# Low rows of batch 0 as unfolded matmuls, and weights before x of batch 2, in an attention and Fourier-mixing kernel

## The chip, the cores and the metric

The kernel runs on one core of one Trainium2 chip. The metric is device time in microseconds (us) of one execution; lower is better. Before the change it took 301.66 us, the median of three runs (300.98, 301.66 and 306.95).

## The reference: what is computed

For each of 8 batches and 8 heads, with x of 512 rows by 64 and a state of 32 rows by 64, two attention reads are made without further projections, put below each other to 544 rows, and the heads side by side to 512 columns. Then comes a Fourier mixing layer with a residual, a normalization and a two-layer network:

```python
a     = softmax(x @ state.T / 8);  xread = a @ state      # 512 rows
a2    = softmax(state @ x.T / 8);  sread = a2 @ x         # 32 rows
X     = concat(xread, sread), heads side by side          # 8 x 544 x 512
u     = X + real(fft(fft(X, axis=1), axis=2))
un    = (u - mean(u)) / sqrt(var(u) + 1e-6)               # over the 512 columns
out   = u + relu(un @ w_ch1) @ w_ch2                      # 512 -> 2048 -> 512
```

## The kernel before, in words

**The transform.** The real part of the two Fourier transforms is made by matmuls with tables of cosines and sines. Symmetry is used twice: rows that mirror each other are added and subtracted ("folded") so that only about half of the row table is needed, and columns are folded again into four quarters (index j = 0 to 3; j = 0 and 1 go with cosines, TC, and j = 2 and 3 with sines, TS). Tiles XF and XR hold the forward and the reversed rows of the reads, in two groups k of 128 rows. The first 32 rows of XR[:, 0] are the "low rows": 32 rows that hold the low end of the sequence and later, written over them, the 32 rows of sread (state_rows). The low rows are folded by themselves: XT is a copy of them, XEl and XOl the sums and differences, XQl[:, j] the four quarters. The second row group of the tables, TC[:, 1] and TS[:, 1], belongs to them. sine_low (L258) writes cosines into rows 32 to 64 of TS[:, 1], which one extra row of XQl needs.

**The opening (batch 0).** open_batch and the batch-0 form of transform are written out by hand, in the order of the lines from L1003 on; each engine runs its instructions in that order. x of batch 0 is loaded and cast to bf16, turned by TensorE (turn_x0, the copies on ScalarE for blocks 0 and 1 and VectorE for 2 and 3), multiplied with the state (score), passed through exp on ScalarE, and read (read, sread). warm(n) issues n matmuls of 128 columns whose result nobody reads. The low rows of batch 0 are folded on GpSimd by low() (L655 to L662). even(k) and odd(k) fold the other rows on VectorE; NC and NS are the negated tables; terms_of(j, part) issues the matmuls of quarter j into the accumulators acc[j] ("gp"), terms_of(j, "low") those of the low rows (4 matmuls of 288 columns in all). out_of copies an accumulator to G; over_d multiplies G with the column table TEO ("yp", L669 and L670). TEO is made on ScalarE by second_sines and second_halves (L264, L268, L269). Then the sums with the reads, the centred rows ub, their turn into unT (turn_u), and layer 1 of batch 0 in 16 quarter steps L[0] to L[15] (L915).

**Batch 1 and the weave.** Between those quarter steps stand the steps of the attention of batch 1: s1 (scores) and r1 (reads), then its transform t1. r1 before the change is, by index: 0 read_low, 1 sread_heads, 2 fold_low (GpSimd), 3 read of rows 0, 4 an early VectorE add of row group 0 plus the GpSimd fold, 5 read of rows 128, 6 state_rows, 7 the last read and fold(). From L1151 on, weave() merges streams of steps by fractions: each stream is given a start and an end between 0 and 1, and its steps are spread evenly between them. M is layer 2 of batch 0 (L969), scores_next the scores of batch 2.

**Transfers.** Nearly all plain transfers are issued by SP's queue, in program order: x of batch b in seven pieces (L140), the states, DMA transposes of x and state for batches 2 and later (xT, sT; turned[b]), and the stores. The weights w1 and w2 are cast from f32 by transfers that GpSimd triggers, four each (L302, L310). A "gate" is a tiny GpSimd operation that reads a tile so that what follows it on GpSimd, or a load that reuses its buffer, comes no earlier. Before the change x of batch 2 is loaded as soon as w1 has landed (L1096), and w2 is triggered after x of batch 2 has landed (L308), in two pairs. States 3 to 7 are loaded into a part of gen2, a buffer that layer 1 of batch 1 takes over as hT.

The softmax here doesn't subtract the row's maximum and nothing guards it: scores larger than these inputs give would overflow.

## Time and profile before

| | |
|---|---|
| runs | 301.66 us (300.98 to 306.95) |
| the profiled execution | 306.59 us, its span 304.8 us |
| TensorE busy | 286.5 us (94%), 2312 matmuls |
| VectorE, ScalarE, GpSimd busy | 181.0, 135.6, 91.3 us |
| first matmul of layer 1, batch 0 | 23.59 us |
| TensorE's last terms matmul, opening | ends 19.97 us; first yp at 20.68 us |
| transfers of weights, trigger to landing | 6.0 to 18.2 us (median 13.2) |
| transposes of xT, batch 2 (four) | SP busy with them 37.06 to 52.6 us |

The profiled execution is one execution on the chip, and its clock times count from the start of its span. A group's line shows engine, line, operation, the tiles written and read, and the time of one. A wait is the idle time of an engine ahead of an instruction, with what ended it. PE is TensorE, DVE VectorE, ACT ScalarE, POOL GpSimd, SP SyncE, which issues transfers.

### The profile page before, as it was taken

The page shows a single profiled execution, that of the slowest core. Times are in us where ns is not written, and L with a number is a line of the kernel's source. Part 1 is how long each engine was busy: PE and PEld are TensorE (multiplying, and loading weights), DVE is VectorE, ACT ScalarE, POOL GpSimd, SP SyncE. Part 2 cuts the span into 40 slices and gives each one's busy share as a digit, 9 for nine tenths or more (in the row PEclk, how much of TensorE's full clock was granted, in tenths as well). Part 3 has the DMA queues.
Part 4 walks back from the last instruction along what each step waited for, and adds up shares of the span by engine and source line. Part 5 has one row for each costly group of instructions (what it writes and reads, how often), then busy time and mean ns, then how long its engine had stood idle before and what let it go on. Part 6 is the DMA issues. An engine that isn't in the chain of part 4 may idle for free.

```text
span 304.8 us, 6036 instructions
## 1 busy us (share of the span) xinstructions
PE 286.5 (94%) x2312; PEld 164.0 (54%) x2343; DVE 181.0 (59%) x443; ACT 135.6 (44%) x254; POOL 91.3 (30%) x217
## 2 busy tenths in 40 slices
PE   5989895799999999999999999999999999999996
PEld 4769792445544555456544555445444544555443
DVE  6876787658688395773827566684668484100012
ACT  5878561565543553345443445245523442333300
POOL 5982744391263033500406022701340031000000
PEclk9999999999999999999999999999999999999999
DMA  8998699974933975459252594363343023600355
GB/s 154 202 204 170 112 149 101 179 159 88 187 96 61 188 146 100 100 93 223 38 129 64 132 178 88 80 127 71 80 96 69 37 69 86 128 12 34 71 134 142
DMA packets 110794, 34.86 MB, mean 114 GB/s; under 512 B 101950, under 2 KB 106302, under 8 KB 110766
## 3 DMA queue, kind: packets, MB, share of 16 engines
q1 hardware_dynamic: 100046, 28.72, 49.0%
q0 software_dynamic: 4224, 4.19, 9.3%
q10 hardware_dynamic: 6496, 1.57, 2.5%
q8 instruction: 18, 0.29, 0.4%
q14 instruction: 10, 0.08, 0.1%
HBM read 22.41 MB, written 14.02 MB: 120 GB/s over the span
## 4 chain that ended last, share of the span: by engine, by line
PE 78%; DMA 11%; SPq 4%; POOL 3%; issue 1%; DVE 1%; ACT 1%; ACTq 0%; POOLq 0%; DVEq 0%
PE po L969 35%; PE ph L905 34%; DMA xT<-xin 5%; SPq L140 3%; DMA s_dram<-in_state_dram 3%; DMA xs<-in_x_dram 3%; PE gp L764 2%; PE po L961 1%; PE yp L669 1%; PE yp L670 1%; POOL w L310 1%; PE xfp L440 1%; PE xrp L440 1%; PE esp L415 1%; PE eTp L427 1%
## 5 line engine op out<-in xcount | busy, mean ns | idle before, releaser
L969 PE MATMUL po<-w,hT 128*128 128x512 bf16 x478 | 121.9, 379 | 5.0 <-DMA w<-in_moe_w_ch_dram 3.6
L907 ACT ACTIVATE hT<-ph 128x512 bf16<-128x512 f32 x112 | 66.8, 597 | 118.5 <-PE ph L905 116.4
L905 PE MATMUL ph<-unT,w 128*128 128x512 bf16 x435 | 112.7, 379 | 0.7
L905 PEld LDWEIGHTS <-w 128*128 128x128 bf16 x576 | 50.6, 98 | 47.4 <-issue 0.4
L969 PEld LDWEIGHTS <-hT 128*128 128x128 bf16 x496 | 46.9, 98 | 50.4 <-issue 4.0
L936 DVE SCALAR_TENSOR_TENSOR ot<-po,rstd,U 128x512 f32<-128x512 f32 (+2 forms) x33 | 24.2, 733 | 53.1 <-PE po L969 51.0
L768 POOL COPY GL<-G 128x128 bf16<-128x128 bf16 x7 | 2.0, 291 | 73.4 <-ACT G L765 73.4
L674 DVE TENSOR_TENSOR U<-yp,XR 128x512 f32<-128x512 f32 x14 | 9.6, 685 | 24.3 <-PE yp L670 24.3
L326 POOL TENSOR_TENSOR rstd<-mv,epst 128x1 f32<-128x1 f32 x34 | 6.7, 196 | 55.1 <-DVE mv L322 55.1
L320 DVE BATCH_NORM_STATS2 st<-U 128x6 f32<-128x512 f32 x32 | 21.7, 679 | 0.0
L327 POOL TENSOR_TENSOR rstd<-rstd,mhalf 128x1 f32<-128x1 f32 x34 | 20.1, 590 | 2.7
L915 PE MATMUL ph<-unT,w 128*128 128x128 bf16 x256 | 16.3, 219 | 0.3 <-ACT unT L835 0.3
L143 POOL CAST xin<-xs 128x512 bf16<-128x512 f32 (+1 forms) x12 | 15.1, 1280 | 2.5 <-DMA xs<-in_x_dram 2.4
L765 ACT CAST G<-gp 128x288 bf16<-128x288 f32 x28 | 13.2, 484 | 5.7 <-PE gp L764 5.7
L915 PEld LDWEIGHTS <-w 128*128 128x128 bf16 x256 | 14.8, 98 | 0.8 <-issue 0.6
L823 DVE TENSOR_SCALAR ub<-U,mv 128x512 bf16<-128x512 f32 x24 | 12.3, 514 | 0.9
L917 ACT ACTIVATE hT<-ph 128x512 bf16<-128x512 f32 x16 | 9.5, 596 | 6.4 <-PE ph L915 6.4
L1001 PE MATMUL warm<-ident 128*128 128x128 bf16 x70 | 7.4, 249 | 3.5 <-POOL xs L287 3.5
L497 POOL COPY XT<-XR 32x514 bf16<-32x514 bf16 x6 | 3.6, 603 | 21.7 <-DVE XR L449 21.7
L449 DVE TENSOR_TENSOR XR<-xrp,rs 128x512 bf16<-128x512 f32 x14 | 9.7, 694 | 0.5
L449 DVE TENSOR_TENSOR XF<-xfp,rs 128x512 bf16<-128x512 f32 x14 | 9.7, 691 | 0.5
L420 ACT ACTIVATE E<-esp 128x512 bf16<-128x512 f32 x14 | 8.4, 599 | 2.6 <-PE esp L415 2.6
(235 smaller groups left out, 371.6 us busy)
## 6 DMA issues: line engine op xcount, KB each, us to landing
xs<-in_x_dram SPq DMA_DIRECT2D x22, 256.0 KB, 3.9
w<-in_moe_w_ch_dram POOLq DMA_DIRECT2D x8, 512.0 KB, 13.2
out_dram<-ot SPq DMA_DIRECT2D x15, 256.0 KB, 3.4
r_dram<-ot SPq DMA_DIRECT2D x14, 256.0 KB, 2.3
out_dram<-r_dram SPq DMA_DIRECT2D x14, 256.0 KB, 3.5
xs<-in_x_dram SPq DMA_DIRECT2D x8, 192.0 KB, 4.8
xs<-in_x_dram ACTq DMA_DIRECT2D x2, 256.0 KB, 5.6
l_dram<-ot SPq DMA_DIRECT2D x2, 256.0 KB, 2.0
```

The source lines that it names most:

```text
L143: copy(xin_bufs[b % 2][:, lo:hi, 1:513], xs_of[b].rearrange("p (i c) -> p i c", i=4)[:, lo:hi])
L320: nc.vector.bn_stats(st6, u)
L327: nc.gpsimd.tensor_tensor(rstd, rstd, mhalf, op=ALU.pow)
L449: nc.vector.tensor_tensor(ov, in0=p[ps, :, 0:256].rearrange("p g (h d) -> p g h d", d=D), in1=rs[ps].unsqueeze(3).to_broadcast([n, 2, 4, D ...
L674: nc.vector.tensor_add(u.rearrange("p (k r) -> p k r", r=2), p.rearrange("p (r k) -> p k r", r=2)[:, 0:u.shape[1] // 2, :], x.rearrange("p ...
L765: nc.scalar.copy(G[:, j, :].rearrange("p (i q) -> p q i", q=2), p[:, 0:NM].rearrange("p (q i) -> p q i", q=2))
L823: nc.vector.tensor_scalar(t, in0=ud, scalar1=mv[:, 0:1], scalar2=None, op0=ALU.subtract)
L905: nc.tensor.matmul(ph[:, o:o + n], lhsT=w1[:, c, f * 128:(f + 1) * 128], rhs=un_of[key][:, c, :], start=(c == 0), stop=(c == DC - 1))
L907: nc.scalar.activation(hT[:, per * i:per * i + per, :].rearrange("p a b -> p (a b)"), ph, AF.Relu, scale=-1.0 / 512 if key == 0 else -1.0 ...
L915: nc.tensor.matmul(ph[:, o:o + 128], lhsT=w1[:, c, f * 128:(f + 1) * 128], rhs=un_of[key][:, c, 128 * r:128 * r + 128], start=(c == 0), st ...
L936: nc.vector.scalar_tensor_tensor(ot[:, cols], in0=po_of[i][:, 0:cols.stop - cols.start], scalar=rstd, in1=u[:, cols], op0=ALU.mult, op1=AL ...
L969: nc.tensor.matmul(po_of[i], lhsT=h_of[key][:, f, i * 128:(i + 1) * 128], rhs=w2[:, f, :], start=(f == 0), stop=(f == FC - 1))
```

## The change

The low rows of batch 0 are no longer folded. A copy XB holds them in order (XB[:, 0], by VectorE) and reversed (XB[:, 1], by GpSimd), with rows 32 to 64 zero, and low_of(j, sign) adds them to the accumulators by matmuls of shifted pieces with the plain or the negated table: 7 for j = 0 and 1 with the plain one, 6 for j = 2 and 3 (two of them of one column), and 8 with the negated. NC and NS now cover both row groups and lie in a work buffer. In the opening, fewer warms are issued, block 1 of x is copied by VectorE, score(1) gets a buffer of tag "t", second_table moves up and sine_low moves behind second_halves. w2 is triggered right behind w1. x of batch 1 is cast after odd(0). For batch 1 the early VectorE add is gone (fold adds both row groups) and the reads stand at other places among the quarter steps. x of batch 2 is loaded behind a gate on the third quarter of w2, and cast behind a gate on the last quarter of the folded rows. The other gates and moves are in the diff. States 3 to 7 get a buffer of their own tag (hTL), and their blocks are made in the weave of batch 1.

```diff
+    stl = wk.tile([128, 1024], F32, name="gen3", tag="hTL", bufs=1)[:, 0:640].rearrange("p (b g d) -> p b g d", b=5, g=2)
+    def states(lo, hi):
+        return stf[:, lo:hi] if lo < 3 else stl[:, lo - 3:hi - 3]
...
+    XB = wk.tile([128, 2, 514], F32, name="XB", tag="U", bufs=5)[0:64].rearrange("p a c -> p (a c)")[:, 0:514].bitcast(BF16).rearrange("p (a c) -> p a c", a=2)
-    NC, NS = [singles.tile([128, NM], BF16, name=n) for n in ("NC", "NS")]
+    NN = wk.tile([128, 2, 514], F32, name="NN", tag="U", bufs=5).rearrange("p a c -> p (a c)")[:, 0:2 * NM].bitcast(BF16)
+    NC, NS = [NN[:, 2 * NM * i:2 * NM * i + 2 * NM].rearrange("p (k c) -> p k c", k=2) for i in range(2)]
+    def minus(o, i):
+        nc.vector.tensor_scalar(o, in0=i, scalar1=-1.0, scalar2=None, op0=ALU.mult)
...
     def clears(i):
         if i == 0:
+            nc.gpsimd.memset(XB[32:64].rearrange("p a c -> p (a c)").bitcast(F32), 0.0)
...
+    def second_weights():
+        for q in range(4):
+            nc.gpsimd.dma_start(out=w2[:, q * 4:(q + 1) * 4, :], in_=w2v[:, q * 4:(q + 1) * 4, :])
-    def load_w2(lo, hi):
-        if lo == 0:
-            nc.gpsimd.tensor_copy(gate, xs_of[2][:, 0:2048:512])
-        for q in range(lo, hi):
-            nc.gpsimd.dma_start(out=w2[:, q * 4:(q + 1) * 4, :], in_=w2v[:, q * 4:(q + 1) * 4, :])
...
         def fold():
-            fold_rows(slice(1, 2) if b < 2 else slice(0, 2))
+            fold_rows(slice(0, 2))
...
         if b < 2:
-            second = [read_low, sread_heads, fold_low, read(0, False, XF[:, 0, 0:512]),
-                      lambda: (fold_rows(slice(0, 1)), fold_low_again()),
-                      read(128, False, XF[:, 1, 0:512]), state_rows,
+            second = [read_low, fold_low, fold_low_again, read(0, False, XF[:, 0, 0:512]), sread_heads,
+                      read(128, False, XF[:, 1, 0:512]), state_rows,
                       lambda: (read(256, True, XR[:, 1, 1:513])(), fold())]
...
-            return lambda: (nc.vector.tensor_copy if si > 1 else nc.scalar.copy)(
+            return lambda: (nc.vector.tensor_copy if si else nc.scalar.copy)(
...
-            p = es[si] = ps0.tile([128, 512], F32, name="esp", tag="e", bufs=2)
+            p = es[si] = ps0.tile([128, 512], F32, name="esp", tag="t" if si == 1 else "e", bufs=2)
...
+        def low_of(j, sign):
+            t, m = XB[:, 0], XB[:, 1]
+            table = ((TC, TS) if sign > 0 else (NC, NS))[j // 2][0:64, 1, :]
+            ws = ({1: [t[:, 0:128], m[:, 1:129], m[:, 257:385], t[:, 256:384]], -1: [t[:, 256:257]]},
+                  {1: [t[:, 0:128], m[:, 1:129], t[:, 256:257]], -1: [m[:, 257:385], t[:, 256:384]]},
+                  {1: [m[:, 1:129], m[:, 257:385]], -1: [t[:, 0:128], t[:, 256:384], t[:, 512:513]]},
+                  {1: [t[:, 384:512], m[:, 129:257]], -1: [m[:, 385:513], t[:, 128:256]]})[j][sign]
+            for w in ws:
+                nc.tensor.matmul(acc[j][0:w.shape[1], 0:NM], lhsT=w, rhs=table, start=False, stop=False)
+            if j == 2 and sign > 0:
+                for c in (128, 384):
+                    nc.tensor.matmul(acc[j][0:1, 0:NM], lhsT=t[:, c:c + 1], rhs=TC[0:64, 1, :], start=False, stop=False)
...
     turn_state()
-    warm(8)
+    second_table()
+    warm(5)
...
     exp2()
-    warm(4)
     copy = turn_x0(0)
...
     read(3)
-    nc.vector.tensor_copy(XTs[0], XRs[0][0:32, 0, :])
-    low()
-    state_blocks(1, 2, nc.gpsimd.tensor_copy)
-    for i in range(4):
-        cast_x(1, lo=i, hi=i + 1)
-    clears(1)
-    warm(6)
+    nc.vector.tensor_copy(XB[0:32, 0], XRs[0][0:32, 0, :])
+    nc.gpsimd.tensor_copy(XB[0:32, 1], XRs[0][0:32, 0, ::-1])
+    second_weights()
+    warm(4)
     read(1)
...
     begin()
-    warm(10)
+    warm(4)
+    low_of(0, 1), low_of(1, 1)
     state_rows()
-    sine_low()
     second_sines()
     second_halves()
-    warm(6)
+    sine_low()
+    low_of(2, 1), low_of(3, 1)
     even(1)
-    nc.vector.tensor_scalar(NC, in0=TC[:, 0, :], scalar1=-1.0, scalar2=None, op0=ALU.mult)
+    minus(NC, TC)
     terms_of(0, 1), terms_of(1, 1)
     odd(1)
-    nc.vector.tensor_scalar(NS, in0=TS[:, 0, :], scalar1=-1.0, scalar2=None, op0=ALU.mult)
-    terms_of(0, "low"), terms_of(1, "low")
+    minus(NS, TS)
+    low_of(0, -1), low_of(1, -1)
     terms_of(2, 1), terms_of(3, 1)
     even(0)
+    low_of(2, -1), low_of(3, -1)
     terms_of(0, 0)
     out_of(0)
     terms_of(1, 0)
     odd(0)
-    terms_of(2, "low"), terms_of(3, "low")
+    nc.gpsimd.tensor_copy(gate, XO0s[:, 0, 0:4])
+    for i in range(4):
+        cast_x(1, lo=i, hi=i + 1)
+    state_blocks(1, 2, nc.gpsimd.tensor_copy)
     terms_of(2, 0)
...
     keep_low()
+    clears(1)
     clear_state(2, 3)
     state_blocks(2, 3, nc.gpsimd.tensor_copy)
     make_mirror()
-    nc.gpsimd.tensor_tensor(gate, xs_of[0][:, 0:4], w1[:, :, 3 * 512], op=ALU.add)
-    load_x(2)
+    clear_state(3, B)
     turned[2, 0]()
-    turn_in_dram(3, B)
...
     L[3]()
     turn_u(1, 1)
+    r1[0]()
+    r1[1]()
+    r1[2]()
+    nc.gpsimd.tensor_copy(gate, w2[:, 8:12, 0])
+    nc.gpsimd.tensor_tensor(gate, xs_of[0][:, 0:4], xs_of[1][:, 0:4], op=ALU.add)
+    load_x(2)
+    L[4]()
     s1[2]()
-    L[4]()
+    r1[3]()
+    L[5]()
     s1[3]()
     turn_u(1, 0)
-    L[5]()
-    r1[0]()
+    r1[5]()
     L[6]()
-    load_w2(0, 2)
-    r1[2]()
-    r1[1]()
-    cast_x(2)
-    turned[2]()
-    load_state(3, B, s_dram)
-    load_x(3)
-    load_w2(2, 4)
+    r1[4]()
     L[7]()
-    r1[3]()
     r1[6]()
     L[8]()
-    r1[4]()
-    r1[5]()
+    r1[7]()
     L[9]()
-    r1[7]()
     L[10]()
     L[11]()
-    clear_state(3, B)
+    nc.gpsimd.tensor_copy(gate, XQs[1][:, 1020:1024])
+    cast_x(2, lo=0, hi=2)
+    cast_x(2, lo=2, hi=4)
+    turned[2]()
+    turn_in_dram(3, B)
+    load_x(3)
+    load_state(3, B, s_dram)
...
-    weave((L[12:], 0, 0.2), (t1, 0.12, 1), ([M[i] for i in (0, 4, 1, 5, 2, 6, 3, 7, 8, 9)], 0.28, 0.99),
-          ([lambda: state_blocks(3, B, nc.gpsimd.tensor_copy)], 0.85, 0.85), (scores_next, 0.6, 1))
+    weave((L[12:], 0, 0.2), (t1, 0.1, 0.95), ([M[i] for i in (0, 4, 1, 5, 2, 6, 3, 7, 8, 9)], 0.25, 0.99), (scores_next, 0.65, 1))
...
-            streams.append(([lambda: (cast_x(b + 2), turned[b + 2]())], 0.2, 0.2))
+            streams.append(([lambda: (b == 1 and state_blocks(3, B, nc.gpsimd.tensor_copy), cast_x(b + 2), turned[b + 2]())], 0.2, 0.2))
```

The undivided copy of unT for the first turned tile (turn_u, batch 0) takes the place of two half copies on ScalarE and VectorE.

## The prediction

> **What bounds the kernel now.** I read the stretches first, then TensorE's waits, then the opening in order of time. The stretches give each engine's busy time in us (number of instructions), the clock, the DMA share and GB/s:
>
> ```profile
> 0.00:10.00 10.00, 6.34 (x84) 6.02 (x85) 7.25 (x33) 5.35 (x11) 6.66 (x41) 1.00 0.89 166
> 10.00:20.00 10.00, 8.53 (x135) 6.25 (x133) 8.34 (x30) 8.29 (x16) 9.18 (x19) 1.00 1.26 202
> 20.00:30.00 10.00, 9.39 (x162) 8.89 (x160) 6.68 (x23) 8.34 (x16) 4.04 (x13) 1.00 0.96 188
> 30.00:40.00 10.00, 8.46 (x173) 7.73 (x169) 7.34 (x14) 5.08 (x9) 7.93 (x13) 1.00 0.73 123
> 40.00:50.00 10.00, 7.74 (x102) 6.25 (x101) 8.34 (x28) 5.24 (x11) 4.61 (x11) 1.00 1.36 120
> 50.00:60.00 10.00, 6.81 (x60) 3.87 (x58) 6.57 (x14) 4.21 (x7) 2.23 (x7) 1.00 1.41 149
> 70.00:305.00 235.00, 229.88 (x1538) 120.20 (x1563) 130.42 (x288) 93.61 (x177) 47.74 (x102) 1.00 0.48 102
> ```
>
> From 70 us on TensorE (first number) is busy for 98%, and the change leaves that work alone. So the end moves by as much as TensorE's work before 60 us moves. There it stands still for 1.5, 2.3 and 3.2 us in the last three ten-us stretches. TensorE's waits between 20 and 62 us (total, times, longest) name the causes:
>
> ```profile
> PE po L969 <- DMA w<-in_moe_w_ch_dram: 3.6, 2, 2.2
> PE esp L415 <- DMA xT<-xin: 1.7, 2, 1.2
> PE xrp L440 <- DVE XF L449: 1.5, 1, 1.5
> ```
>
> Two waits for w2, two for the transposed x of batch 2, one for VectorE: 6.8 us. The opening (ScalarE, start and duration) decides whether something new comes in their place:
>
> ```profile
> 15.19 0.60 ACT L640 CAST XR<-hdp 32x512 bf16<-32x512 f32 x1
> 15.82 0.53 ACT L258 ACTIVATE TS<-gen,halfpi 32x288 bf16<-32x288 f32 x1
> 16.38 0.72 ACT L264 ACTIVATE TEO<-gen,pi_pos 128x512 bf16<-128x512 int32 x1
> 17.13 0.72 ACT L268 ACTIVATE TEO<-TEO,sg 128x512 bf16<-128x512 bf16 x1
> 17.88 0.41 ACT L269 ACTIVATE TEO<-TEO 1x256 bf16<-1x256 bf16 x1
> ```
>
> The low sine (L258) is done at 16.35 today, before TensorE wants a sine table (17.4).
>
> **What the Trainium skill says.** (1) "GPSIMD Engine Reference", Key points: GpSimd shares its SBUF interfaces with VectorE, which hurts VectorE's instructions with two SBUF inputs. The trace agrees: the 128x514 add of L513 takes 2.01 us while GpSimd casts x(2) (35.13 to 37.03), 0.49 us otherwise. (2) "DMA: Bandwidth & Descriptors", Queues, rings and completion order: each DMA engine takes turns between its queues packet by packet. The trace agrees: four xT transposes take SP 15.56 us beside w2, 5.23 us later. (3) "TensorE: Matmul & The Clock Gate", Part 1: an idle window of about 3.4 us halves TensorE's clock. No idle of that length follows the start here.
>
> **Opening, part by part.** *Reads:* removing warms, copying block 1 of x on VectorE instead of ScalarE and giving score(1) a "t" buffer lets score(1) start after that copy. VectorE's copy takes the place of the 0.42 us table step at 10.08, so it ends near 10.6; the last exp of the opening starts at 11.2 instead of 11.85, and the tables TC and TS are ready 0.65 earlier (14.0, 14.6). Gain so far 0.6.
>
> *Low rows:* eight small GpSimd operations (3.8 us, 13.48 to 17.26) go. New are a memset of XB (32x514 words; 264 words take 0.34 and 1320 take 1.19, so 0.54) ahead of the w1 triggers, and one reversed copy (as L497 on GpSimd, 0.61). Triggers of w1: 9.74+0.54 = 10.28 to 13.6 (3.33 as now); copy 13.6 to 14.2. TensorE gets 21 matmuls of 288 columns in place of 4. Three of 288 columns show 0.54 and one 0.28, so 0.13 each: 17 more are 2.2 us. The 12 warms of 16 that go between the first of them and the terms only filled idle time, so they pay for nothing. minus() now covers both row groups, 576 elements instead of 288 (0.22 undisturbed today): bounded by 0.22 and twice that, I take 0.3 each; the first is hidden behind the wait below, the second counts in it.
>
> *What is moved:* low_of(0,1) and low_of(1,1), 7 x 0.13 = 0.9, now stand ahead of the state rows on TensorE and wait for the reversed copy: 14.25 to 15.15. The state rows' matmuls follow (0.40 as now), end 15.55 instead of 15.16. ScalarE then does copy 0.60, second_sines 0.72, second_halves 0.72 and 0.41, and only then sine_low 0.53, with 0.03 between each: 15.6 + 3.1 = 18.7. The next instruction on TensorE, low_of(2,1), reads TS[0:64, 1], of which sine_low writes rows 32 to 64. That XB is zero there does not remove the dependence. So TensorE waits from 15.55 to 18.7, with terms_of(0,1) queued behind (16.39 today). On VectorE, minus(NS, TS) reads the same rows and waits too, with even(0) and odd(0) behind it: 18.7 + 0.3 + 1.6 (17.28 to 18.86 today) = 20.6.
>
> TensorE after 18.7: 23 matmuls of 288 columns at 0.13 and 18 of 144 at 0.06 are 4.1 us, so the last term ends near 22.9, not 19.97; even(0) and odd(0) at 20.6 are hidden by it. From there to yp 0.71 and from yp to the first matmul of layer 1 2.91 us as today (20.68 to 23.59), 0.15 more for the undivided copy of unT (0.59 against 0.37): 26.7 instead of 23.59. GpSimd's casts of x(1) (2.29) and state blocks (1.49) now start at odd(0)'s end, 20.6+0.2, and end at 24.6; today's turn of batch 1 would want them at 24.4 to 24.9, so they just fit. **+3.1 us.** Bounds, since no row shows this wait: if TensorE finds the table ready, the earlier reads leave -0.5; if the clock also halves in the gap, 3.4 us at half rate add an estimated 1.7 (from that page's window).
>
> **Middle.** *Reads without the wait:* the split add leaves; both rows are added in fold, with the cast of x(2) gated to after fold (XQs[1]). -1.5 us. The longer add in fold (0.49 more) is covered by L[9] to L[14] on TensorE (6 x 1.06); without that cover it would cost its 0.5.
>
> *w2 behind w1:* four triggers at 14.2 to 17.4 on GpSimd, behind which only the x(1) casts wait, later anyway. The w queue moved 0.93 MB in 15 to 20 us when it ran nearly alone; 0.44 of the 4.19 MB are in by 15 us with today's w1, so all is in at 15 + 3.75/0.186 = 35 us, and first used at 44. Both waits go: -3.6.
>
> *x(2) behind w2:* GpSimd's gate waits for the third quarter, about 33; nothing else is queued there until fold ends. From gate to data took 9.6 us (issue 22.22, seen 31.80), so 43. Fold ends at about 46.5 (r1[7] near 39.4, then VectorE's chain of 6.6 as now plus 0.5), the two half casts end 47.7 and 48.6, SP issues four transposes of 1.3, landing in 2.8: the first pair at 51.8, the second at 54.3. TensorE wants the first near 54.2 + 3.1 - 1.5 - 3.6 + 0.6 (the stream begins at 0.65) = 52.8 and the second about a us later. -1.7, of which 0.3 comes back.
>
> *States 3 to 7* lie in another buffer, so layer 1 of batch 1 no longer waits for their blocks (ScalarE's hT waited 1.6 us for GpSimd, TensorE stood 0.63 us in 60 to 70): -0.4. The blocks move ahead of the cast of x(3); 3 us of GpSimd (2.98 at 61.10 today), finished near 69 with scores wanted after 73: 0.
>
> *SP's queue* loses the seven issues of x(2) between 22.2 and 29.4 and gets them back near 33 to 40, where it stood idle (32.2+0.8 to 37.06) or in slow transposes. Behind the xT transposes (now over by 53, as today 52.6) come turn_in_dram (0.84), the seven issues of x(3) (8.45 beside w2, 5.3 elsewhere) and then load_state (0.54), whose data must land before the blocks near 64: it is issued at 60 and lands about 3 later, as the other gen loads (2.6). The first store of out waits behind it as it does today (61.85). GpSimd's clears(1) (0.66) and clear_state(3,B) (1.19) move into gaps of 26 to 33 us. All 0; uncovered they would cost their own length.
>
> **The sum.** On the profiled execution (306.59 us, span 304.8, 1.79 around it): 306.59 + 3.1 - 1.5 - 3.6 - 1.7 + 0.3 - 0.4 = 302.8. That execution lies 4.93 above the median of 301.66, and the DMA waits counted off are 5.3: perhaps the median run has hardly any of them. Then from the median: 301.66 + 3.1 - 1.5 + 0.3 - 0.4 = 303.2. Both sums meet, so I take **302.8**: much is removed from the profile, little from the median.
>
> **Rivals.** *A, ScalarE is not late* (0.20): TensorE finds the low sine ready, or the wait is under a us. For it: reads end 0.6 earlier. Against: four ScalarE operations now precede it. Layer 1 starts near 23.2: 299.3. With all waits gone and DMA otherwise quick as well, it passes under 295.6: 0.08.
>
> *B, x(2) comes too late, slower than before* (0.14): the gate puts the load after w2. First scores can run 9.6 + 0.95 + 1.3 + 2.8 = 14.7 us after the gate, so it decides from a gate at 38.1. If w2 drains at 0.5 MB in 5 us, as between 40 and 45 today, the third quarter lands at 47 and TensorE stands about 9 us: 311.5. Over 2% slower begins at a gate near 43. For it: state reloads and transposes of sT run beside w2. Against: they are small.
>
> *C, the clock or the triggers* (0.11): TensorE's clock halves in the 3.1 us gap (304.5), or eight outstanding weight transfers hold GpSimd in its triggers and the casts of x(1) come 4 us late (306 to 308).
>
> The likeliest (0.55) has its own range 300.5 to 305. The range 298.5 to 308 leaves out A's low end and most of B. A measurement of this kernel tells about 2% (6 us) from no change: faster by more 0.08, within 0.73, slower by more 0.19 (B and the worst of C).
>
> **What would show it.** Right: ScalarE's L258 ends near 18.7, with a TensorE wait of about 3 us just ahead of it for TS; first matmul of layer 1 near 26.7; no wait on w; the add in fold near 1 us. Wrong: layer 1 starts before 24.5 (A); a wait on xT over 1 us, or a gate released after 38 us (B); a clock under 1.0 near 20 us, or w triggers longer than 0.8 us (C).

## The result and the profile after

The changed kernel takes 314.29 us (median of 4 executions, 314.0 to 315.23). Against the kernel before the ratio is 1.0436, with a 95% interval of 1.0392 to 1.0479: 4% slower, and above the predicted range. The profiled execution took 314.48 us, its span 312.7 us. Most executions of the kernel before lie near 301 or near 306 us; ratios here leave out those more than 1.5% above the fastest, and the one profiled for the prediction, 306.59, was one of these.

The stretches of the changed kernel, with the columns as before (PE, PEld, DVE, ACT, POOL, then clock, DMA share, GB/s):

```profile
10.00:20.00 10.00, 6.44 (x95) 3.72 (x91) 6.47 (x28) 6.86 (x12) 7.07 (x11) 0.83 1.25 202
20.00:30.00 10.00, 9.89 (x51) 4.93 (x50) 1.20 (x5) 2.47 (x5) 4.69 (x14) 0.50 1.24 205
40.00:50.00 10.00, 10.00 (x208) 9.58 (x205) 6.72 (x18) 6.73 (x12) 2.54 (x8) 1.00 0.52 107
60.00:70.00 10.00, 7.36 (x49) 3.73 (x47) 3.58 (x8) 5.80 (x12) 1.88 (x5) 0.83 0.91 192
80.00:90.00 10.00, 8.21 (x67) 4.97 (x69) 6.17 (x16) 5.31 (x11) 1.08 (x3) 1.00 0.83 173
90.00:312.00 222.00, 217.94 (x1454) 113.66 (x1477) 121.70 (x269) 86.05 (x162) 46.78 (x99) 1.00 0.44 100
```

Between 20 and 30 us TensorE counts as busy for 9.89 of 10 us and gets through 51 matmuls, where before it was 162 (not all of the same kinds): the granted clock (third number from the right, as a share of full speed) is 0.50. A high busy share here is slow work, not much work. Between 40 and 50, where the waits for w2 stood, TensorE is never idle. Its waits from 14 to 100 us:

```profile
PE gp L747 <- ACT TS L270: 3.1, 1, 3.1
PE gp L771 <- DVE XQ L531: 1.4, 1, 1.4
PE eTp L437 <- ACT E L430: 0.9, 1, 0.9
PE esp L425 <- DMA xT<-xin: 0.8, 1, 0.8
PE tp L839 <- ACT E L430: 0.7, 1, 0.7
PE xrp L450 <- ACT ET L438: 0.6, 1, 0.6
```

No wait on w and none of the 1.5 us for XF is left. In their place stand one long wait for the sine table and five that the prediction did not have. ScalarE's opening, to be read beside the ScalarE lines of before in the prediction:

```profile
15.60 0.60 ACT L648 CAST XR<-hdp 32x512 bf16<-32x512 f32 x1 [1.31 <-issue]
16.10 0.71 ACT L276 ACTIVATE TEO<-gen,pi_pos 128x512 bf16<-128x512 int32 x1
16.84 0.72 ACT L280 ACTIVATE TEO<-TEO,sg 128x512 bf16<-128x512 bf16 x1
17.60 0.41 ACT L281 ACTIVATE TEO<-TEO 1x256 bf16<-1x256 bf16 x1
18.02 0.53 ACT L270 ACTIVATE TS<-gen,halfpi 32x288 bf16<-32x288 f32 x1
```

The low sine (L270) comes last and ends at 18.55, where 18.7 was predicted. What follows on TensorE is not as predicted:

```profile
18.61 0.64 PE L747 MATMUL gp<-TS,XB 64*128 64x288 bf16 x2 [3.09 <-ACT TS L270]
...
23.93 1.58 PE L747 MATMUL gp<-NN,XB 64*128 64x288 bf16 x5
...
32.44 0.77 PE L917 MATMUL ph<-unT,w 128*128 128x128 bf16 x11 [0.29 <-DVE unT L840]
```

The wait is 3.09 us. But layer 1 (L917) starts at 32.44, not at 26.7. The clock is at half from about 16.6 to 30.2 us:

```profile
15.00:16.00 1.00, 0.52 (x5) 0.32 (x5) 0.69 (x5) 0.40 (x1) 1.00 (x2) 1.00 1.22 198
16.00:17.00 1.00, 0.00 (x0) 0.00 (x0) 0.00 (x0) 0.97 (x3) 1.00 (x2) 0.79 1.22 200
17.00:18.00 1.00, 0.00 (x0) 0.00 (x0) 0.00 (x0) 0.97 (x2) 0.07 (x1) 0.50 1.24 207
...
28.00:30.00 2.00, 1.90 (x14) 1.33 (x13) 0.54 (x2) 1.52 (x3) 1.23 (x5) 0.50 1.24 206
30.00:31.00 1.00, 1.00 (x15) 0.91 (x14) 0.92 (x3) 0.22 (x1) 0.87 (x4) 0.88 1.24 207
```

**Two marks that split every run.** Mark A is the first matmul of layer 1 of batch 0. Mark B is a group of layer-2 matmuls that TensorE reaches after 0.16 us of idle time. In an execution of the kernel before that took 301.22 us (e3, span 299.4) they are:

```profile
23.59 2.16 PE L915 MATMUL ph<-unT,w 128*128 128x128 bf16 x32 [0.29 <-ACT unT L835]
...
83.80 0.81 PE L969 MATMUL po<-w,hT 128*128 128x512 bf16 x3 [0.16 <-issue]
```

| us, profiled execution | A | B | B - A | span | span - B |
|---|---|---|---|---|---|
| before, as profiled for the prediction | 23.59 | 89.22 | 65.63 | 304.8 | 215.6 |
| before, e3 | 23.59 | 83.80 | 60.21 | 299.4 | 215.6 |
| changed | 32.44 | 97.39 | 64.95 | 312.7 | 215.3 |
| e1, sine first | 28.58 | 92.42 | 63.84 | 307.7 | 215.3 |
| e2, gap filled | 27.93 | 93.00 | 65.07 | 309.1 | 216.1 |
| e6, old opening | 23.63 | 88.04 | 64.41 | 303.5 | 215.5 |
| e7, blocks behind cast | 31.80 | 96.00 | 64.20 | 311.4 | 215.4 |
| e8, old weave | 34.44 | 95.80 | 61.36 | 311.1 | 215.3 |
| e10, middle mended | 23.57 | 87.54 | 63.97 | 302.8 | 215.3 |
| e12, states early | 23.59 | 84.48 | 60.89 | 300.4 | 215.9 |
| e13, no single columns | 26.61 | 90.23 | 63.62 | 305.5 | 215.3 |
| e14, change mended | 25.94 | 84.69 | 58.75 | 300.1 | 215.4 |
| e15, x(2) ahead | 23.59 | 83.35 | 59.76 | 298.7 | 215.4 |

After B all of them take 215.3 to 216.1 us, so the kernels differ by more than 0.8 us only ahead of B. A and B come from one execution each; differences of medians are given beside them. Against e3 the changed kernel loses 13.3 us of span: 8.85 ahead of A (the opening) and 4.7 between A and B (the middle), less 0.3 behind B. The two losses are taken apart in what follows.

### The profile page after: what moved, and what is told of

Its sections match the earlier page's. It is cut to its first block, busy times and chain, and to the rows that moved or that the text cites. A ratio compares the mean times of both kernels' runs of the same rounds, so it can differ in the third digit from the quotient of the medians.

```text
span 312.7 us, 6017 instructions
## 1 busy us (share of the span) xinstructions
PE 294.6 (94%) x2307; PEld 165.8 (53%) x2338; DVE 179.9 (58%) x443; ACT 135.2 (43%) x252; POOL 88.9 (28%) x214
## 4 chain that ended last, share of the span: by engine, by line
PE 69%; DVE 3%; POOL 2%; DMA 2%; SPq 1%; issue 1%; POOLq 0%
PE po L971 32%; PE ph L907 29%; PE gp L771 2%; PE po L963 1%; PE yp L668 1%; PE yp L667 1%; POOL stb L168 1%; DVE U L672 1%; DMA xT<-xin 1%; SPq L370 1%; DVE st L330 1%; DMA unT<-ub 1%; PE xrp L450 1%; PE esp L425 1%; DVE ub L830 1%
## 5 line engine op out<-in xcount | busy, mean ns | idle before, releaser
L917 PE MATMUL ph<-unT,w 128*128 128x128 bf16 x256 | 15.9, 219 | 0.3 <-DVE unT L840 0.3
L148 POOL CAST xin<-xs 128x512 bf16<-128x512 f32 (+2 forms) x13 | 15.5, 1212 | 2.5 <-DMA xs<-in_x_dram 2.4
L917 PEld LDWEIGHTS <-w 128*128 128x128 bf16 x256 | 14.8, 98 | 0.6 <-issue 0.4
L672 DVE TENSOR_TENSOR U<-yp,XF 128x510 f32<-128x510 f32 x14 | 9.5, 677 | 0.0
L458 DVE RECIPROCAL rs<-xrp 128x8 f32<-128x8 f32 x14 | 2.9, 204 | 11.4 <-PE xrp L450 11.4
```

The lines of the kernel that those rows point to most:

```text
L148: copy(xin_bufs[b % 2][:, lo:hi, 1:513], xs_of[b].rearrange("p (i c) -> p i c", i=4)[:, lo:hi])
L672: nc.vector.tensor_add(u.rearrange("p (k r) -> p k r", r=2), p.rearrange("p (r k) -> p k r", r=2)[:, 0:u.shape[1] // 2, :], x.rearrange("p ...
L917: nc.tensor.matmul(ph[:, o:o + 128], lhsT=w1[:, c, f * 128:(f + 1) * 128], rhs=un_of[key][:, c, 128 * r:128 * r + 128], start=(c == 0), st ...
```

## The experiments

**e3_before_again** repeats the kernel before unchanged. 

> The kernel before, unchanged, for a second profile of it. If the waits of TensorE for w2 and for xT (5.4 us in the first profile, at 306.6 us) are what lies between its executions near 301 and those near 306.6, a profile near 301 to 302 us shows less than 2 us of them; if it shows them in full, the 5 us lie elsewhere (in the opening, or after 60 us).

Median 301.49 us of 18 executions (301.02 to 305.98). The profiled one, 301.22, has no wait on w. Of the waits that the prediction counts off it has these (20 to 110 us):

```profile
PE xrp L440 <- DVE XF L449: 0.7, 1, 0.7
...
PE esp L415 <- DMA xT<-xin: 0.3, 1, 0.3
```

B - A is 60.21 there and 65.63 in the execution that the prediction was built on: 5.4 us, about the size of the four DMA waits of the latter (5.3). An execution near the median, then, does not have these waits, and of the 1.5 us for XF it has half. Why these waits come in some executions only is not shown.

**Which half loses what: e6_old_opening.** Everything up to the first layer 1 as before, the rest as changed.

```diff
-    low_of(0, 1), low_of(1, 1)
     state_rows()
+    sine_low()
     second_sines()
     second_halves()
-    sine_low()
...
+    terms_of(0, "low"), terms_of(1, "low")
```

> The kernel before up to the first layer 1 (folded low rows, the old place of the low sine, the old warm-ups), and the changed kernel from there on (reads, weights, x of batch 2, states, weave). Theory: the middle of the change costs 4 to 5 us by itself (waits of TensorE for ScalarE's exponentials near 57 to 64 us, for the fold of batch 2 and for xT near 80), so 305 to 307, with the opening at the old 23.6 us. Rival, that these waits come only from the late and half-clocked opening: 299.5 to 302, reads 1.5 us shorter and no new wait.

306.26 us (ratio 1.0153, 1.009 to 1.0215). A is at 23.63 and the clock at 1.00 up to B, and the waits of the middle are those of the changed kernel to 0.2 us:

```profile
PE gp L766 <- DVE XQ L525: 1.4, 1, 1.4
PE eTp L432 <- ACT E L425: 0.9, 1, 0.9
PE xrp L445 <- ACT ET L433: 0.8, 1, 0.8
PE esp L420 <- DMA xT<-xin: 0.8, 1, 0.8
PE tp L834 <- ACT E L425: 0.7, 1, 0.7
```

So the middle loses its 4 to 5 us by itself, and the opening the other 8 (medians, 314.29 - 306.26).

### The opening

**e1_sine_first.** The low sine back ahead of the other sines.

```diff
     state_rows()
+    sine_low()
     second_sines()
     second_halves()
-    sine_low()
```

> The changed kernel with sine_low put back ahead of second_sines, nothing else. Theory W (the place of sine_low makes TensorE wait 3.1 us, and the wait halves its clock for 13 us): sine_low ends at 16.8 instead of 18.6, the wait shrinks to about 1.3 us, the clock stays at 1.0, the first matmul of layer 1 comes near 24.5 instead of 32.44, and the time falls by about 8 us, to 306.5. Rival L (the low matmuls of 64 rows keep the clock down whatever the wait): the clock near 20 us is still 0.5, layer 1 starts near 30.5, the time is 311 to 313.

313.18 us (309.5 to 313.85; ratio 1.0345, 1.0245 to 1.0444), so most executions gain little. The profiled one is the fastest, 309.5 us; the mean clock of the whole execution is 0.989 in it and 0.978 in the three others, as in the changed kernel (0.973 to 0.984). Its wait is down to 1.29 us, and still the clock falls, after the wait:

```profile
16.00:17.00 1.00, 0.28 (x2) 0.09 (x1) 0.29 (x1) 0.95 (x3) 0.98 (x2) 1.00 1.24 204
17.00:18.00 1.00, 1.00 (x10) 0.46 (x9) 0.96 (x7) 0.97 (x2) 0.00 (x0) 1.00 1.22 204
18.00:19.00 1.00, 1.00 (x10) 0.43 (x7) 0.39 (x3) 0.59 (x2) 0.53 (x2) 0.70 1.23 198
19.00:20.00 1.00, 1.00 (x7) 0.45 (x5) 0.00 (x0) 0.00 (x0) 1.00 (x3) 0.50 1.24 203
```

A late sine is not the whole cause: with a wait of less than half the length the clock is lost as well, for 6 to 7 us here. By the mean clocks it is longer in the three others (0.978 of some 312 us means about 14 us at half clock in all, an estimate).

**e2_gap_filled.** The late sine stays; 44 matmuls that nobody reads fill the wait.

```diff
     state_rows()
+    warm(44)
     second_sines()
```

> The changed kernel with 44 warm matmuls of 128 columns put into the gap in which TensorE waits for sine_low (2.9 us at 66 ns), so that the wait's end stays and only the idleness goes. Theory W: low_of(2,1) still starts at 18.6, but at the full clock; the terms take 4.1 us instead of 9.4, layer 1 starts near 26.7 as predicted, and the time falls by about 5.7 us, to 308.5; the wait alone is then worth about 2 to 3 us of the difference to the run with sine_low first. Rival L: the clock halves all the same, time within 1 us of 314.3.

310.15 us (ratio 1.027, 1.0195 to 1.0345), 4.1 us less than the changed kernel by the medians. The clock is 1.00 up to 59 us. TensorE's marks:

```profile
18.72 0.40 PE L747 MATMUL gp<-TS,XB 64*128 64x288 bf16 x2 [0.53 <-ACT TS L270]
...
27.93 1.95 PE L917 MATMUL ph<-unT,w 128*128 128x128 bf16 x32 [0.29 <-DVE unT L840]
```

The sine is as late as before, the start of layer 1 4.5 us earlier. This separates the two: at A the clock cost 4.5 us in these two executions. A comes 1.2 us behind the predicted 26.7.

**e9_low_128_rows** asks whether 64 rows of weights cause this 1.2: XB and the table are taken with all 128 partitions, 64 of them zero.

```diff
-            table = ((TC, TS) if sign > 0 else (NC, NS))[j // 2][0:64, 1, :]
+            table = ((TC, TS) if sign > 0 else (NC, NS))[j // 2][:, 1, :]
```

> As e2_gap_filled (the changed kernel with 44 warm-ups in TensorE's wait for the low sine), but the low rows' matmuls take all 128 partitions of weights and table, the other 64 zeros in the weights. Theory: the 64-row weights are what spaces these matmuls at 0.17 to 0.24 us instead of 0.13, so the 20 or so of them after the wait take about 1 us less and the first matmul of layer 1 comes near 26.8 instead of 27.9: 309. Rival, that they are spaced by something else (the weights' short columns, accumulating into one tile): unchanged at 310.1.

309.92 us, and the matmuls are spaced as in e2 (five of 288 columns in 0.97 us in both). It is not the rows. e2's weight loads, by their shape, show a part of what it is:

```profile
19.05 0.08 PEld L750 LDWEIGHTS <-XB 64*1 64x1 bf16 x2 [0.23 <-issue]
19.38 0.11 PEld L747 LDWEIGHTS <-XB 64*128 64x128 bf16 x2 [0.25 <-issue]
...
22.26 0.32 PEld L747 LDWEIGHTS <-XB 64*1 64x1 bf16 x3 [0.24 <-issue]
22.82 0.36 PEld L714 LDWEIGHTS <-SS 128*128 128x128 bf16 x4 [0.24 <-issue]
```

Nearly wherever weights go from 128 columns to one or back (a group's line bears the name of its first), the loads stand about 0.24 us, mostly with no wait shown.

**e13_no_single_columns** leaves the low rows' products with one column of weights out of the computation: row 0 of the sums lacks their share.

```diff
-            for w in ws:
+            for w in ws[:-1] if ws[-1].shape[1] == 1 else ws:
...
-            if j == 2 and sign > 0:
-                for c in (128, 384):
-                    nc.tensor.matmul(acc[j][0:1, 0:NM], lhsT=t[:, c:c + 1], rhs=TC[0:64, 1, :], start=False, stop=False)
```

> As e2_gap_filled, but the products of the low rows with a single column of weights are left out (row 0 of the sums lacks their share). Theory: the surplus of 1.2 us over the predicted 26.7 for the first matmul of layer 1 is the change from 128 columns of weights to one and back, at each of which weight loads stand 0.24 us; without them layer 1 starts near 26.8 and the time is 309. Rival, that the matmuls of the low rows with 128 columns are slow themselves: under 0.4 us less.

308.23 us, 1.9 less than e2. From the sine to layer 1 it is 8.25 us (18.36 to 26.61), where e2 has 9.21 and the prediction 8.0. So the four single-column products behind the sine cost 1.0 us there, 0.24 each. The prediction had them at 0.13 each, so only about half of this is the price of the changes. With them left out the stream from the sine to the warm-ups takes 4.46 us (5.42 in e2), and the prediction's unit prices, less these four, give 3.6. So its unit prices were too low for the rest as well. The kernel before shows it too:

```profile
16.39 0.22 PE L716 MATMUL gp<-NC,SS 128*128 128x144 bf16 x1 [0.80 <-DVE NC L1057]
...
19.80 0.61 PE L1001 MATMUL warm<-ident 128*128 128x128 bf16 x8
```

From the first of these lines to the second run 13 matmuls of 288 columns and 18 of 144, with no wait of TensorE shown among them; they take 3.41 us, and the unit prices give 2.8.

### The middle

**e8_old_weave.** The changed kernel with the old fractions.

```diff
-    weave((L[12:], 0, 0.2), (t1, 0.1, 0.95), ([M[i] for i in (0, 4, 1, 5, 2, 6, 3, 7, 8, 9)], 0.25, 0.99), (scores_next, 0.65, 1))
+    weave((L[12:], 0, 0.2), (t1, 0.12, 1), ([M[i] for i in (0, 4, 1, 5, 2, 6, 3, 7, 8, 9)], 0.28, 0.99), (scores_next, 0.6, 1))
```

> The changed kernel with the first weave's fractions as before (transform 0.12 to 1, layer 2 0.28 to 0.99, scores 0.6 to 1 instead of 0.1 to 0.95, 0.25 to 0.99, 0.65 to 1). Theory: the waits of TensorE for ScalarE and VectorE at 57 to 64 us come of the transform of batch 1 being drawn forward into the place of its roots; later fractions take 1 to 2 us of them and the second clock drop away: 311 to 313. Rival, that they come of VectorE's chain being late whatever the fractions: 314 or slightly more.

312.39 us (311.1 to 313.29): 1.9 less. Of TensorE's three waits for ScalarE two are gone (tp, xrp) and the third is 0.6 instead of 0.9. B - A falls by 3.6, to 61.36. So the fractions are worth between 1.9 us (medians) and 3.6 (marks); these runs do not say more closely. (A itself lies at 34.44 in this execution and at 31.80 in e7, with the same opening. In e8 the low sine already ended 1.5 us later than in the changed kernel, 20.08 against 18.55. From the sine's end to A it is 14.4 us in e8, 13.9 in the changed kernel and 13.3 in e7.) As I read the traces, the new fractions brought the transform of batch 1 forward, ahead of where VectorE has its statistics ready, and ScalarE's exponentials stood in line behind operations that waited for these. In e6 ScalarE stands 1.0 us for the statistics at 52.62, and the exponential that TensorE waits for runs right behind:

```profile
52.62 0.72 ACT L823 ACTIVATE ub<-U,mv 128x512 bf16<-128x512 f32 x1 [1.00 <-DVE mv L327]
53.24 0.58 ACT L425 ACTIVATE E<-esp 128x512 bf16<-128x512 f32 x1
```

**e7_blocks_behind_cast.** On GpSimd the cast and the transposes of x(3) go ahead of the blocks of states 3 to 7. The transposes of batch 3's state then read blocks that are not yet written, so this kernel leaves that state out of batch 3's scores.

```diff
-  (b == 1 and state_blocks(3, B, nc.gpsimd.tensor_copy), cast_x(b + 2), turned[b + 2]())
+  (cast_x(b + 2), turned[b + 2](), b == 1 and state_blocks(3, B, nc.gpsimd.tensor_copy))
```

> The changed kernel with one order turned round on GpSimd: cast and transposes of x(3) ahead of the state blocks 3 to 7. Theory: the 1.4 us wait of TensorE for the fold of batch 2 and the 0.8 us for xT of batch 3 come from the blocks that push the cast into the fold; without them 314.3 - 2.2 = 312.1. Rival, that the blocks now collide with the fold in the cast's place: the fold's add stays near 2 us and the time at 314.

313.11 us (312.87 to 313.27), 1.2 less; by the marks about half of this lies ahead of A, where nothing was changed. The wait for xT is gone, the one for XQ stays (1.5): the cast (72.69 + 1.89) now ends before VectorE's fold of batch 2 begins (75.26), and the blocks (75.61 + 4.30) lie beside it. Three of the fold's operations take 1.09 to 1.20 us instead of 0.7 each, where in the changed kernel one took 2.27 beside the cast. Either of GpSimd's two works stretches the fold from that place. The theory was right on xT and wrong on XQ.

**e11_reads_alone.** The kernel before with only the reads changed.

```diff
-            fold_rows(slice(1, 2) if b < 2 else slice(0, 2))
+            fold_rows(slice(0, 2))
...
     L[6]()
     load_w2(0, 2)
-    r1[2]()
     r1[1]()
+    r1[2]()
     cast_x(2)
...
```

> The kernel before with the reads of batch 1 alone changed: both fold adds in fold, the fold of the low rows in one go, the reads in the changed order; weights, x of batch 2 and weave as before. Prediction's step: 1.5 us off, 300.0. Rival, that the gain is slack, because the transform behind it waits for the sums of batch 0 and the weave's order anyway, or that the wait was the cast of x(2) on GpSimd and only moves with it: 301.5 or more.

302.47 us, ratio 1.001 (0.9993 to 1.0027): nothing gained. The rival holds. (None of its 14 executions is over 302.71, while 5 of the 19 of the kernel before beside it are over 306; why is open.) The wait for XF is 1.0 us, at another instruction, and new ones come with it: 0.6 for XQ in hdp, 1.0 for xT of batch 2. My reading, not tested apart: as long as the cast of x(2) lies among the reads, it delays one thing or another.

**e4_weights_order_alone** puts w2 behind w1, x(2) behind w2 and the cast behind the fold, in the kernel before.

```diff
+    for q in range(4):
+        nc.gpsimd.dma_start(out=w2[:, q * 4:(q + 1) * 4, :], in_=w2v[:, q * 4:(q + 1) * 4, :])
...
-    load_w2(0, 2)
...
-    cast_x(2)
-    turned[2]()
...
+    nc.gpsimd.tensor_copy(gate, XQs[1][:, 1020:1024])
+    cast_x(2, lo=0, hi=2)
+    cast_x(2, lo=2, hi=4)
+    turned[2]()
```

> The kernel before with only the order of transfers changed: w2 triggered behind the casts of x(1) on GpSimd (near 21 us), x of batch 2 loaded behind a gate on the third quarter of w2, its cast, its transposes and the loads behind it moved after fold; opening, places of the reads and fractions of the weave as before. Theory H (the waits for w2 and xT cover a chain of VectorE and ScalarE work of batch 1 and 2, which then becomes the wait): the waits on w2 are gone, but TensorE stands between 45 and 65 us for ScalarE or VectorE instead, and of 5.4 + 1.5 us only 2 to 4 come back: 303 to 304.5 against the profiled 306.6, or 300 to 302 if the executions near 301 never had them. Rival D (the waits are pure transfer time and come back in full): 299.5 to 300.5, with TensorE idle for less than 1 us between 40 and 65 us. The casts of x(2) away from fold also show whether the add of row group 0 takes 0.5 us instead of 2.01 with its place unchanged.

305.23 us (ratio 1.0108, 1.0017 to 1.0199). No wait on w or xT, and the split add of the fold takes 0.43 us at its old place instead of 2.01: it was the cast of x(2), not the place of the add, that made it long. But the run was spoilt by my edit. It left the memset of states 3 to 7 behind that cast, VectorE waited 3.5 us for it and TensorE 3.9 us for VectorE. The changed kernel has this memset early.

**e5_order_clear_early** is e4 with the memset early.

```diff
+    clear_state(3, B)
     turned[2, 0]()
...
-    clear_state(3, B)
     state_ones(2, B)
```

> The kernel before with the second weights behind the first and x of batch 2 behind them, as in e4_weights_order_alone, but with the memset of the states 3 to 7 (clear_state) early, where the changed kernel has it. Theory: the 305.2 of e4 was the 3.5 us that VectorE waited for that memset and the clock that fell after it; without it 300.5 to 302, no wait on w2, and no single time near 306. Rival, that the late load of x(2) itself costs (transposes of x(2) later than TensorE wants them): 304 to 306 again, with a wait on xT over 1 us in layer 1's neighbourhood near 52 to 58 us.

306.64 us (ratio 1.0146). Neither account held. Up to 60 us TensorE has one wait that e3 doesn't have, 0.5 us for ScalarE, and then it waits 2.0 us for xT, of batch 3 and not of batch 2; from 70 to 90 us its mean clock is 0.91. GpSimd's blocks of states 3 to 7 wait 2.8 us for the load of these states, which is now issued behind the transposes of x(2).

**e10_middle_mended.** e6 with the old fractions, the blocks back in the first weave, and the states loaded ahead of x(3).

```diff
-    load_x(3)
     load_state(3, B, s_dram)
+    load_x(3)
...
+          ([lambda: state_blocks(3, B, nc.gpsimd.tensor_copy)], 0.85, 0.85), (scores_next, 0.6, 1))
```

> As e6_old_opening (the old opening, the changed kernel from layer 1 on), with the first weave's fractions as before, the blocks of the states 3 to 7 back in that weave at 0.85, and the load of these states ahead of that of x(3). Theory: the loss of 4.7 us in the middle lies in these two placements, so 301 to 302.5, with no wait for XQ in batch 2 over 0.3 and none of TensorE for ScalarE's exponentials over 0.7; and if the 1.5 us of the shorter reads reach the end, 300. Rival, that the late x(2) or the weights' order costs as well: 303.5 or more, with waits for xT that stay.

305.09 us (ratio 1.0103): the rival's side. Up to 58.3 us it runs 0.36 ahead of e3, then it loses 4.1 us up to B. GpSimd and TensorE show the same chain as e5 (in brackets the idle time before it and what ended it):

```profile
57.89 2.98 POOL L168 CAST stb<-gen 32x640 bf16<-32x640 f32 x4 [2.52 <-DMA gen<-s_dram]
...
64.54 1.88 POOL L148 CAST xin<-xs 128x2048 bf16<-128x2048 f32 x1
```

```profile
71.51 0.29 PE L420 MATMUL esp<-sT,xT 128*128 128x64 bf16 x4 [1.13 <-DMA xT<-xin]
72.80 0.29 PE L420 MATMUL esp<-sT,xT 128*128 128x64 bf16 x4 [0.99 <-DMA xT<-xin]
```

In e3 the blocks stand at 55.69 and the cast at 62.34, 2.2 us earlier, and the fold's add takes 0.70 us, not the 1.71 that it takes here beside the cast.

**e12_states_early.** e10 with the states' turn in DRAM and their load early on SP's queue.

```diff
     turned[2, 0]()
+    turn_in_dram(3, B)
+    load_state(3, B, s_dram)
```

> As e10_middle_mended, with the turn of the states 3 to 7 in DRAM and their load early on SP's queue, ahead of x of batch 2, where the kernel before has the turn. In e10 GpSimd's blocks of these states waited 2.5 us for that load (57.89 instead of 55.69), the cast of x(3) behind them came 2.2 us later than in the kernel before, fell into the fold's add (1.71 us instead of 0.70) and TensorE waited 2.1 us for xT of batch 3. Theory: that chain is what is left of the middle's loss, so 301 to 302, blocks near 55.5, no wait for xT over 0.3. Rival, that the cast is late because x(3) itself is loaded late behind x(2): 304 or more, with the waits for xT still there.

303.84 us (301.82 to 305.23, 22 executions; ratio 1.0045, 1.002 to 1.007), 1.3 below e10 and between the two accounts. The profiled execution, 302.18, is among the fastest. The chain of batch 3 is gone (cast at 63.26, add 0.69 us). But now the load of the states waits on SP until 39.28 for the turn, the load of x(2) behind it starts at 39.8, GpSimd's casts of x(2) wait 2.1 and 2.3 us for data, and TensorE 2.0 us for xT of batch 2.

**e15_x2_ahead.** e12 with the load of the states behind that of x(2).

```diff
-    load_state(3, B, s_dram)
...
     load_x(2)
+    load_state(3, B, s_dram)
```

> As e12_states_early (the old opening, the mended middle), with the load of the states 3 to 7 behind the load of x(2) on SP's queue instead of ahead of it. In e12 that load stood on SP until 39.3 us, behind the states' turn in DRAM, and held x(2) back: the casts of x(2) waited 2.1 and 2.3 us and TensorE 2.0 us for xT. Theory: with x(2) issued from 36 us the casts start near 43.6, nothing is left of the waits, and the 1.5 us of the shorter reads reach the end: 300.0 to 300.7, below the kernel before, with no execution near 306. Rival, that x(2) lands late anyway because the weights fill the DMA engines until 38 us: 302 to 304.

300.56 us (299.76 to 301.66, 6 executions). The kernel before took 305.53 beside it (11 executions, most of them near 306); the ratio is 0.9897 (0.9829 to 0.9964). Its longest waits from 14 to 110 us:

```profile
PE gp L718 <- DVE NC L1061: 0.8, 1, 0.8
PE eTp L432 <- ACT E L425: 0.6, 1, 0.6
```

No wait on w, XF, XQ or xT is left, and this is the fastest version here, the only one with an interval below the kernel before. The gain is small: against e3 it is 0.45 us between A and B and 0.7 us of span, not the expected 1.5. Most of the ratio is that none of its six executions is near 306.

**e14_change_mended.** The whole change, with the low sine first, 20 matmuls in the gap, and the middle of e12.

```diff
     state_rows()
+    warm(20)
+    sine_low()
     second_sines()
     second_halves()
-    sine_low()
...
```

> The whole change with both repairs: the low sine ahead of the other sines and 20 warm-ups in TensorE's wait, and the middle as in e12_states_early. Theory: the losses are separate and add up, so e2's 310.1, less 1.5 to 1.8 for the earlier sine, less the 4.7 of the middle: 303.5 to 304.5, with a clock of 1.0 until 60 us and layer 1 from 26 us. Rival, that the middle's waits return when the opening is late: 306 or more.

302.16 us (301.8 to 304.23, 12 executions; ratio 1.0018, 0.9988 to 1.0048): no slower than before, and 1.3 better than the best I expected. Its marks:

```profile
25.94 1.95 PE L917 MATMUL ph<-unT,w 128*128 128x128 bf16 x32 [0.29 <-DVE unT L840]
...
84.69 0.81 PE L971 MATMUL po<-w,hT 128*128 128x512 bf16 x3 [0.16 <-issue]
```

The clock is 1.00 in every stretch up to 100 us. The opening costs 2.35 us more than the old one, and from A to B it takes 1.46 us less than e3. Part of this is no gain. e12 has the same middle behind the old opening, and its B is only 0.2 us earlier (84.48): starting later, e14 comes to the places where e12 waits 2.0 us for xT when the data are there. In sum 12 us come back by other places for a few operations and by 20 matmuls that nobody reads.

e1 and e14 differ up to A only in these 20 matmuls. In both the low sine ends near 16.7 and the product behind it starts at 16.73; with them the clock stays at 1.00 and A is at 25.94, without them it halves and A is at 28.58.

## Why the prediction was wrong, step by step

**Where the 11.7 us lie.** 314.48 was measured in the profiled execution and 302.8 predicted; the base of both accounts is the execution of 306.59. The opening was priced at +3.1 and cost 8.85: 5.75 more. The middle was priced at -6.9 and gave -0.7 (64.95 against 65.63): 6.2 less. (Behind B 0.3 came back.) So two steps failed, one in each half.

**The late sine: right.** 18.55 against 18.7, a wait of 3.09 us against 3.15. The four triggers of w2 took 3.04 us on GpSimd, the longest 0.83, just at the mark set for that rival; but they were over at 17.07 and the casts of x(1) began at 20.39, behind their own gate, so the triggers held nothing up.

**What follows the sine: the step that failed in the opening.** "TensorE after 18.7: 23 matmuls of 288 columns at 0.13 and 18 of 144 at 0.06 are 4.1 us." They took 9.4 us (18.61 to about 28.0). At full clock (e2) they take 5.4: the unit prices were 1.3 too low, of which about 0.6 shows in the kernel before already and 0.45 is the change to single columns and back (e13). The remaining 4 us are the half clock. The likeliest case left this out with one sentence, "No idle of that length follows the start here": a wait of 3.15 us was held to be safe because an idle window of about 3.4 us was thought to be needed. Rival C had it, priced at 1.7 us: 3.4 us at half rate, from the length of the idle window. Measured, it is 4.5 us at A. Two things were wrong in that estimate. It let the clock return about one window after work resumed, while here it stayed at 0.50 for 11.6 us of almost unbroken matmuls. And it made the loss hang on the length of the wait, while e1 lost the clock with 1.29 us. The Trainium skill, "TensorE: Matmul & The Clock Gate", Part 1, has the clock halve after an idle window of about 3.4 us and return after about 3.4 us of sustained work; this trace disagrees with both as I used them (1.29 us in e1, 11.6 us in the changed kernel), and the measurement decides. That the 12 warm-ups taken out there "only filled idle time, so they pay for nothing" was the costly sentence: e1 and e14 show that such matmuls in this wait pay for the clock, 2.6 us at A. Whether the 12 would have been enough was not run. Of the opening's 8.85 us, then, 4.5 are the clock (changed kernel to e2), 2.0 are the wait together with the place of the sine (27.93 in e2, 25.94 in e14), 1.0 the single columns, and the last 1.4 are not taken apart; most of the added matmuls are in them.

**w2 and xT: right waits, wrong base.** The waits went as said. But of the 5.3 us almost none was to be had from an execution near 301, as e3 shows. The prediction's second sum, from the median, saw this possibility. That both sums met was taken as support, but they share every other term. Their meeting says only that the first profile lay above the median (4.93) by about its DMA waits (5.3), which e3 bears out; it says nothing for the shared terms, and those failed. One sign of rival B came as well: the gate on w2 was passed at 42.16, not near 33. The prediction had nothing else on GpSimd there. But the fold of the low rows of batch 1 stands ahead of the gate and waited for VectorE until 39.23, behind the late opening; in e14, with layer 1 from 25.94, the gate is passed at 35.66. TensorE did not wait for x(2) because of it.

**Reads, -1.5: too high, and right only when the rest is mended.** In e3 the wait to be removed is 0.7 us, and e15, where it is gone, gains 0.45 between A and B. In the changed kernel other waits swallowed it, and alone (e11) it moved elsewhere.

**The middle's other terms: the step that failed there.** Three of them were put at nothing or not priced, and with them the middle loses 4 to 5 us (e6); e15 differs from e6 in these three alone and takes 5.7 us less.

*The states' blocks, 0:* they and the cast behind them are GpSimd's work beside VectorE's fold of batch 2; the first add of sums takes 2.27 us instead of 0.69, TensorE waits 1.4 for XQ and 0.8 for xT. The prediction asked only whether the blocks are ready before the scores want them, not what GpSimd runs beside. It had itself cited the Trainium skill, "GPSIMD Engine Reference", Key points, for just that effect; the trace agrees again. (The -0.4 for their own buffer rested on a wait of TensorE that was not there: its idle time from 60 to 70 us before was 0.4 for VectorE's XR and 0.2 for ScalarE's ET.)

*The weave's fractions, not priced:* they were a few hundredths in the diff. e8 shows 1.9 us for them by the medians, 3.6 by the marks.

*SP's queue, 0:* hidden, not free. In the changed kernel nothing of it shows. Once the rest was mended (e10, e12, e15), the order of three loads on that queue decided over 4.5 us (305.09 to 300.56).

**The second fall of the clock**, 0.50 from 65 to 67 us in the changed kernel, follows the waits of the middle. The profiled execution of e6 has these waits without it. But two of e6's four executions have a mean clock of 0.994 and take 307.1 us, and the two at 1.00 take 305.3 and 305.4. So this fall may cost up to 1.7 us of the middle's loss; no run separates it. Why the clock stays down through work is open too: the matmuls there are short, with single columns of weights and a weight-load share of about half, and it comes back 0.6 us (e1) to 3.5 us (e8) after the start of the first dense run of 128 columns; no run told these apart.

## What to carry to other kernels

Look at the granted clock of every stretch before pricing a wait of TensorE, and give up warm-up matmuls in front of a wait only after asking what else keeps the clock; here, among short matmuls, a wait of 1.29 us cost 2.6 (e1 against e14). Build the sum on an execution near the median: waits that only other executions have cannot be removed from it. When an operation is moved to another engine's quiet time, ask what the neighbour engine does at that moment, and look at every load behind it on the queue.

## What the runs showed of the hardware

- The clock fell to half after 1.29 us of idle time (e1), less than 2 us behind its end, and stayed there for 7 to 14 us (e1, changed kernel) while TensorE counted as busy; with 44 or 20 matmuls in that time (e2, e14) it did not fall there.
- The clock column alone is not enough. It says 1.00 from 3 to 5 us, where 11 warm-ups of 128 columns take 1.35 us (changed kernel, from 3.46), 0.12 each; in e2 44 of them take 2.63, 0.06 each. Why the first ones are slow is not shown; the spacing of equal matmuls is the second thing to look at.
- 64 or 128 rows of weights make no difference to the spacing of matmuls (e2 and e9: five in 0.97 us). At a change between 128 columns of weights and one, weight loading stands about 0.24 us (e2), and a product with a single column takes 0.24 us of TensorE's time among others of 0.13 (e13 against e2).
- Beside GpSimd's cast single adds of VectorE take 1.71 us (e10) and 2.27 us (changed kernel) instead of 0.7; beside its block copies three operations take 1.09 to 1.20 us (e7).
